# Retention and FFN on one core: two key casts on another engine, and one step's outputs inside an output block

## The chip, the cores and the metric

One core of one Trainium2 chip. A core has five engines with an instruction stream of their own: TensorE (PE; its weight loads are listed as PEld), VectorE (DVE), ScalarE (ACT), GpSimd (POOL) and SyncE (SP), which here only issues DMAs. Each works its stream strictly in order; between engines, semaphores hold an instruction until what it needs is done. The metric is the device time of one execution in microseconds, as a median over runs.

## The reference

A decaying linear attention (retention), 4 batches of 8 heads, 768 tokens, head width 64, followed by a multiplicative feed-forward network on the 3072 tokens:

```python
for t in range(S):
    state = gamma[None, :, None, None] * state + np.einsum('bhd,bhe->bhde', k[:, :, t], v[:, :, t])
    y[:, :, t] = scale * np.einsum('bhd,bhde->bhe', q[:, :, t], state)
...
a = x @ w1            # x: (3072, 512), from y; w1, w2: (512, 1024)
b = x @ w2
h = a * b @ w3        # w3: (1024, 1024)
return (h @ w_out)    # w_out: (1024, 512)
```

## The kernel before

**Tiles.** The sequence is cut into 24 chunks of 128 tokens (`n`; six per batch). In a chunk the recurrence is done as matrices: `scores(n)` multiplies keys and queries (L437) into two PSUM banks, VectorE multiplies each by the causal mask into `am` (L442); `kv(n)` makes the chunk's addition to the state (L460), VectorE adds the old state (L468) and GpSimd scales (L469); `outputs(n)` adds masked scores times values (L477, L478) and state times queries (L480) in one bank, which VectorE scales into the transposed FFN input `xt` (L485). Decay factors are folded into the scaled values `vp`, the factors `YS` and the state scale `GS`.

The keys enter the scores transposed. `transposes(n)` fills `kp` (L426 and L230 from TensorE's transposes, L411 and L412 from a DMA transpose). The DMA makes it for chunk 6 and for chunks from 8 on (`by_dma`), the rest TensorE.

**The FFN.** w3 and w_out are multiplied into one matrix `W3O` in the prologue, so a block of tokens needs `a_unit` (w1, L508, then a ScalarE copy, L518), `b_unit` (w2, L508, then a VectorE product with it into `ht`, L524) and `o_unit`: eight matmuls against `W3O` (L534), a ScalarE eviction (L539) and a DMA to the output (L541). `o_unit` takes an optional function `between`, called after the fourth matmul. Most blocks have 256 tokens; the second and third have 128.

**Order.** All order is written by hand (manual schedule). The first four chunks are unrolled with the weight preparation (the prologue); from chunk 4 on `step(n)` runs, with FFN units kept in a queue `fill`, from which it pulls a share by cost at three places. In step 5 the first unit that is pulled after `outputs(5)` is the output block of `ffn[1]`.

**Around the first edit.** The keys and values of chunks 2 and 3 come as one load for the pair, token pairs side by side in a partition. `pair_casts(n, moved, names, eng)` casts the half that stays on its partitions (by default on GpSimd) and the half that moves to the other 64 (by default on VectorE): for keys one copy of 64 partitions by 512 elements (L313), for values two multiplications (L318). In the prologue (L729 to L731) both chunks' keys are cast, then TensorE has the next matmuls of w1 (L719), the query transposes (L366), three more w1 blocks, and `transposes(2)`, which needs both halves of chunk 2. TensorE then goes on with w1, the transposes of chunk 3, `scores(2)`, the first part of w2 and `outputs(2)`. The two value multiplications on VectorE stand between the two masks of `scores(2)`; GpSimd does four in the meantime (two each for chunks 2 and 3).

**Around the second edit.** In step 5 TensorE has `scores(5)`, one `b_unit`, `outputs(5)`, the output block of `ffn[1]`, `scores(6)`, and FFN units of the next block, which read `xt` of chunks 4 and 5. `transposes(6)` issues no TensorE work: it is the two ScalarE copies L411 and L412, from the DMA transpose that step 4 issued.

Of the kernel before, what the change touches and what calls it, by code (L numbers as in the profile page):

```python
# [18 lines left out]
def kernel(  # L19
# [11 lines left out]
    nc = tc.nc  # L31
# [210 lines left out]
    def bank(tag, shape, dtype, name):  # L242
        return (ps_t if tag == "psT" else ps_at).tile(shape, dtype, tag=tag, name=name)
# [59 lines left out]
    def pair_casts(n, moved, names="kv", eng=None):  # L303

        m, c = divmod(n, 2)
        rows = slice(c * 64, c * 64 + 64)
        t = 1 - c if moved else c
        to = slice(t * 64, t * 64 + 64)
        eng = eng or (nc.vector if moved else nc.gpsimd)
        if n not in k16s:  # L310
            k16s[n] = att.tile([128, 512], HP, tag="k16", name="k16", bufs=3)
        if "k" in names:
            eng.tensor_copy(  # L313
                k16s[n][to, :].rearrange("i (h d) -> i h d", d=D),
                pair_in["k", m][rows, :].rearrange("i (h t d) -> i h t d", t=2, d=D)[:, :, t, :],
            )
        for r in range(2 if "v" in names else 0):
            eng.tensor_tensor(  # L318
                VP[n % 3][to, :, r, r * 64 : r * 64 + 64],
                pair_in["v", m][rows, :].rearrange("j (p s t e) -> j p s t e", s=2, t=2, e=64)[:, :, r, t, :],  # L320
                VS2[rows, t, :].rearrange("j (p s) -> j p s", s=2)[:, :, r].unsqueeze(2).broadcast_to((64, NP, 64)),
                MULT,
            )
# [9 lines left out]
    def casts(n):  # L333
        if n >= NSTEP:
            return
        k32, v32 = chunk_in.pop(n)
        if n % 2 == 0:
            q_cast(n // 2)
        k16 = att.tile([128, 512], HP, tag="k16", name="k16", bufs=3)
        nc.gpsimd.tensor_copy(k16[:, :], k32[:, :])  # L340
        vp = VP[n % 3]

        for r in range(2):
            nc.gpsimd.tensor_tensor(  # L344
                vp[:, :, r, r * 64 : r * 64 + 64],
                v32[:, :].rearrange("j (p s e) -> j p s e", s=2, e=64)[:, :, r, :],
                VS[:, :].rearrange("j (p s) -> j p s", s=2)[:, :, r].unsqueeze(2).broadcast_to((128, NP, 64)),
                MULT,
            )
        k16s[n] = k16  # L350
# [30 lines left out]
    def by_dma(n):  # L381

        return n >= DT0 and n != DT0 + 1

    def dma_transposes(n):

        if n < DT0 or n >= NSTEP:
            return
        if by_dma(n):
            kT = att.tile([128, NP, 128], HP, tag="kT", name="kT", bufs=2)  # L390
            nc.sync.dma_start_transpose(kT[:, :, :], k16s[n][:, :])
            kTs[n] = kT
        if n % 2 == 0:
            qT = att.tile([128, 2, NP, 128], HP, tag="qTd", name="qTd", bufs=2)
            nc.sync.dma_start_transpose(
                qT[:, :, :, :].rearrange("p t a i -> p (t a) i"), q16s.pop(n // 2)[:, :]
            )
            qTd[n // 2] = qT

    def queries(n, p):  # L400
        if n < DT0:
            return qTs[n][:, p, :]
        c = n % 2
        return qTd[n // 2][:, :, p, c * 64 : (c + 1) * 64]

    def transposes(n, tag="psT"):
        if n >= NSTEP:
            return
        if by_dma(n):
            kT, kp = kTs.pop(n), KP[n % 2]  # L410
            nc.scalar.copy(kp[0:64, :, 0, :], kT[0:64, :, :])  # L411
            nc.scalar.copy(kp[64:128, :, 1, :], kT[64:128, :, :])  # L412
            return
        transposes_front(n, tag)
        transposes_back(n)

    def transposes_front(n, tag):
        k16 = k16s[n]
        ps = bank(tag, [128, NP, 128], HP, "psT")
        for p in range(NP):  # L420
            nc.tensor.transpose(ps[:, p, :], k16[:, p * 128 : (p + 1) * 128], ident16[:, :])
        kTs[n] = ps

    def transposes_back(n):
        kp, ps = KP[n % 2], kTs.pop(n)
        nc.scalar.copy(kp[0:64, :, 0, :], ps[0:64, :, :])  # L426
        cast_to(kp[64:128, :, 1, :], ps[64:128, :, :], False)

    def scores(n, tags=("psA0", "psA1"), between=None):
        kp = KP[n % 2]  # L430
        am = att.tile([128, NP, 2, 128], HP, tag="am", name="am")
        for half in range(2):
            ps = bank(tags[half], [128, 2, 2, 128], FP, "psA")
            for i in range(2):
                p = half * 2 + i
                for r in range(2):
                    nc.tensor.matmul(  # L437
                        ps[:, i, r, :], lhsT=kp[:, p, r, :], rhs=queries(n, p), start=True, stop=True
                    )
            if half and between:  # L440
                between()
            nc.vector.tensor_tensor(  # L442
                am[:, half * 2 : half * 2 + 2, :, :].rearrange("j p s i -> j (p s) i"),
                ps[:, :, :, :].rearrange("j p s i -> j (p s) i"),
                (keep2 if n < 4 else keep)[:, :].unsqueeze(1).broadcast_to((128, 4, 128)),
                MULT,
            )
        ATs[n] = am

    def kv(n, tag="psK", eng=nc.gpsimd):  # L450
        k16, vp = k16s.pop(n), VP[n % 3]
        c = n % NCH
        if c == NCH - 1:
            return None
        ps = bank(tag, [128, NP, 128], FP, "psK")
        for p in range(NP):

            rhs = vp[:, p, :, :].rearrange("j s e -> j (s e)")
            rhs = bass.AP(rhs.tensor, rhs.offset, [list(rhs.ap[0]), [192, 2], [1, 64]])
            nc.tensor.matmul(  # L460
                ps[:, p, :], lhsT=k16[:, p * 128 : (p + 1) * 128], rhs=rhs, start=True, stop=True
            )
        t16 = att.tile([128, NP, 128], HP, tag="t16", name="t16")
        if c == 0:
            nc.vector.tensor_tensor(t16[:, :, :], ps[:, :, :], GS[:, :, :], MULT)
        else:
            s32 = att.tile([128, NP, 128], FP, tag="s32", name="s32")
            nc.vector.tensor_tensor(s32[:, :, :], ps[:, :, :], Tst[0][:, :, :], ADD)  # L468
            eng.tensor_tensor(t16[:, :, :], s32[:, :, :], GS[:, :, :], MULT)  # L469
        return t16  # L470

    def outputs(n, tag="psY"):
        am, vp = ATs.pop(n), VP[n % 3]
        c = n % NCH
        ps = bank(tag, [128, NP, 128], FP, "psY")
        for p in range(NP):
            nc.tensor.matmul(ps[:, p, :], lhsT=vp[:, p, 0, :], rhs=am[:, p, 0, :], start=True, stop=False)  # L477
            nc.tensor.matmul(ps[:, p, :], lhsT=vp[:, p, 1, :], rhs=am[:, p, 1, :], start=False, stop=(c == 0))  # L478
            if c > 0:
                nc.tensor.matmul(ps[:, p, :], lhsT=Tst[0][:, p, :], rhs=queries(n, p), start=False, stop=True)  # L480
        if n % 2 == 0:
            XT[n // 2] = xpool.tile([128, NP, 256], HP, tag="xt", name="xt")

        order = "p a (t i) -> p a t i"
        nc.vector.tensor_tensor(  # L485
            XT[n // 2][:, :, n % 2 * C : (n % 2 + 1) * C].rearrange("p a (i t) -> p a t i", t=2),
            ps[:, :, :].rearrange(order, t=2), YS[:, :, :].rearrange(order, t=2), MULT,
        )
# [107 lines left out]
    fill = Queue()  # L596
# [3 lines left out]
    def step(n):  # L600

        ready = n * C
        share = fill.available(ready) / (2 - n % 2)
        if n >= DT0 - 2:
            casts(n + 2)
        scores(n)
        fill.pull(share * 0.25, ready)
        t_new = kv(n)
        if n < DT0 - 2:
            casts(n + 2)  # L610
        dma_transposes(n + 2)
        load_chunk(n + 4)
        if n % 2:
            q_transposes((n + 1) // 2)
        if n == 4:
            transposes(5)
        fill.pull(share * 0.25, ready)
        outputs(n)
        Tst[0] = t_new
        if n != 4:  # L620
            transposes(n + 1)
        fill.pull(share * 0.5, ready)

# [44 lines left out]
    cast_w3(7, w3_st[7])  # L668
    q_cast(0)
    pair_casts(0, False, "k")  # L670
    pair_casts(1, False, "k")
    pair_casts(0, False, "v")
# [28 lines left out]
    ffn = [Ffn(a, b - a) for a, b in zip(bounds, bounds[1:])]  # L701
# [26 lines left out]
    by_rows(W1, ps, 1)  # L728
    for n in (2, 3):  # L729
        pair_casts(n, False, "k")  # L730
        pair_casts(n, True, "k")  # L731
    by_rows(W1, ps, 2)
    q_back = q_transposes(1, True)
    q_back(0)
# [92 lines left out]
```

## Time and profile before

| | |
|---|---|
| median of 10 runs | 196.7 us (195.85 to 198.07) |
| the profiled execution | 196.37 us |
| its span (first to last recorded instruction) | 194.3 us |
| TensorE busy, share of the span | 186.2 us, 96% |
| VectorE busy | 118.0 us, 61% |
| ScalarE busy | 99.0 us, 51% |
| GpSimd busy | 85.7 us, 44% |
| moved by DMA | 40.54 MB, 209 GB/s mean |

A row of a timeline has the start in us from the span's start, the length in us, engine, source line, operation, what is written and read, the shape, and how many such instructions are merged; in brackets, how long the engine sat idle before it, and what ended that. The releaser is inferred: where the engine named had long been done, it was something else, often a DMA. Matmuls overlap in the pipeline, so the starts of two that follow each other say what one costs: 0.055 us for 128 columns, 0.216 for 512 here.

### The profile page before, as it was taken

The page shows a single profiled execution, that of the slowest core. Times are in us where ns is not written, and L with a number is a line of the kernel's source. Part 1 is how long each engine was busy: PE and PEld are TensorE (multiplying, and loading weights), DVE is VectorE, ACT ScalarE, POOL GpSimd, SP SyncE. Part 2 cuts the span into 40 slices and gives each one's busy share as a digit, 9 for nine tenths or more (in the row PEclk, how much of TensorE's full clock was granted, in tenths as well). Part 3 has the DMA queues.
Part 4 walks back from the last instruction along what each step waited for, and adds up shares of the span by engine and source line. Part 5 has one row for each costly group of instructions (what it writes and reads, how often), then busy time and mean ns, then how long its engine had stood idle before and what let it go on. Part 6 is the DMA issues. An engine that isn't in the chain of part 4 may idle for free.

```text
span 194.3 us, 4696 instructions
## 1 busy us (share of the span) xinstructions
PE 186.2 (96%) x1777; PEld 141.0 (73%) x1777; DVE 118.0 (61%) x221; ACT 99.0 (51%) x191; POOL 85.7 (44%) x146
## 2 busy tenths in 40 slices
PE   6899999779999999999999999999999999999993
PEld 2445567568796889778877887788778877887752
DVE  3225498699586768657565766575657665753220
ACT  5478465582444455455545554555455545533322
POOL 7600378738764747385242643852426432200000
PEclk9999999999999999999999999999999999999999
DMA  6999999999999999999999989969979931111104
GB/s 206 360 390 392 301 399 320 366 284 220 210 180 233 211 235 243 170 242 209 267 189 189 212 186 224 207 155 255 204 182 198 206 95 25 57 54 54 43 29 148
DMA packets 85030, 40.54 MB, mean 209 GB/s; under 512 B 61328, under 2 KB 80016, under 8 KB 85008
## 3 DMA queue, kind: packets, MB, share of 16 engines
q1 hardware_dynamic: 85008, 40.25, 88.2%
q8 instruction: 14, 0.23, 0.5%
q14 instruction: 8, 0.07, 0.2%
HBM read 29.36 MB, written 6.29 MB: 184 GB/s over the span
## 4 chain that ended last, share of the span: by engine, by line
PE 84%; DMA 7%; DVE 3%; ACT 3%; POOL 1%; issue 1%; SPq 0%; POOLq 0%
PE psF L508 39%; PE psO L534 20%; DMA stg<-in_moe_w_dram 7%; PE psA L437 5%; PE psW L280 3%; PE psY L477 3%; PE psY L478 2%; PE psY L480 2%; PE psK L460 2%; PE psW L259 1%; PE psZ L634 1%; DVE am L442 1%; ACT w L230 1%; PE psF L719 1%; PE psW L293 1%; PE psG L508 1%
## 5 line engine op out<-in xcount | busy, mean ns | idle before, releaser
L508 PE MATMUL psF<-xt,w 128*128 128x256 f16 (+1 forms) x736 | 85.0, 266 | 0.0
L508 PEld LDWEIGHTS <-w 128*128 128x128 f16 x768 | 68.2, 98 | 7.2
L524 DVE TENSOR_TENSOR ht<-pa,psF 128x256 f16<-128x256 f32 x88 | 36.6, 416 | 22.1 <-PE psF L508 12.9
L518 ACT COPY pa<-psF 128x256 f32<-128x256 f32 x84 | 31.3, 372 | 33.8 <-PE psF L508 33.3
L442 DVE TENSOR_TENSOR am<-psA,keep 128x512 f16<-128x512 f32 x48 | 31.0, 685 | 22.9 <-PE psA L437 22.8
L534 PE MATMUL psO<-w3o,ht 128*128 128x512 f16 x184 | 43.1, 379 | 0.0
L469 POOL TENSOR_TENSOR t<-s,GS 128x512 f16<-128x512 f32 x15 | 19.3, 1284 | 43.0 <-DVE s L468 38.8
L539 ACT ACTIVATE osb<-psO 128x512 f32<-128x512 f32 x23 | 13.7, 597 | 37.5 <-PE psO L534 37.5
L534 PEld LDWEIGHTS <-ht 128*128 128x128 f16 x184 | 17.9, 98 | 17.2 <-DVE ht L768 0.2
L344 POOL TENSOR_TENSOR vp<-v,VS 128x256 f16<-128x256 f32 x40 | 23.8, 617 | 5.2 <-PE psY L478 2.2
L327 POOL CAST q<-q 128x1024 f16<-128x1024 f32 x12 | 12.7, 1057 | 24.2 <-DMA q<-in_q_dram 24.2
L485 DVE TENSOR_TENSOR xt<-psY,YS 128x512 f16<-128x512 f32 x24 | 17.8, 743 | 3.5 <-PE psY L480 3.2
L477 PE MATMUL psY<-am,vp 128*128 128x128 f16 x96 | 16.8, 219 | 0.9 <-ACT kp L230 0.5
L478 PE MATMUL psY<-am,vp 128*128 128x128 f16 x96 | 16.7, 219 | 0.4 <-DVE vp L318 0.4
L437 PEld LDWEIGHTS <-kp 128*128 128x128 f16 x192 | 12.5, 98 | 4.9 <-ACT kp L230 0.9
L340 POOL CAST k<-k 128x512 f16<-128x512 f32 x20 | 12.3, 614 | 5.3 <-PE psK L460 2.3
L468 DVE TENSOR_TENSOR s<-psK,t 128x512 f32<-128x512 f32 x16 | 11.0, 688 | 3.0 <-PE psK L460 2.7
L251 DVE COPY w3t<-psW 128x1024 f16<-128x1024 f16 x8 | 5.4, 688 | 11.1 <-PE psW L259 8.7
L437 PE MATMUL psA<-qTd,kp 128*128 128x128 f16 x144 | 11.1, 219 | 0.0
L480 PE MATMUL psY<-qTd,t 128*128 128x128 f16 x60 | 10.8, 219 | 0.0
L411 ACT COPY kp<-kT 64x512 f16<-64x512 f16 x17 | 10.5, 618 | 0.6 <-DMA kT<-k 0.2
L478 PEld LDWEIGHTS <-vp 128*128 128x128 f16 x96 | 9.4, 98 | 1.9 <-POOL vp L318 0.9
(80 smaller groups left out, 195.6 us busy)
## 6 DMA issues: line engine op xcount, KB each, us to landing
stg<-in_moe_w_dram SPq DMA_DIRECT2D x16, 512.0 KB, 7.9
q<-in_q_dram SPq DMA_DIRECT2D x12, 512.0 KB, 5.4
out_dram<-osb SPq DMA_DIRECT2D x23, 256.0 KB, 2.5
k<-in_k_dram SPq DMA_DIRECT2D x20, 256.0 KB, 5.2
v<-in_v_dram SPq DMA_DIRECT2D x20, 256.0 KB, 5.1
stg<-in_moe_w_out_dram SPq DMA_DIRECT2D x4, 512.0 KB, 7.8
stg<-in_k_dram SPq DMA_DIRECT2D x2, 512.0 KB, 10.7
stg<-in_v_dram SPq DMA_DIRECT2D x2, 512.0 KB, 8.2
```

The lines of the kernel that those rows point to most:

```text
L344: nc.gpsimd.tensor_tensor(vp[:, :, r, r * 64 : r * 64 + 64], v32[:, :].rearrange("j (p s e) -> j p s e", s=2, e=64)[:, :, r, :], VS[:, :]. ...
L437: nc.tensor.matmul(ps[:, i, r, :], lhsT=kp[:, p, r, :], rhs=queries(n, p), start=True, stop=True)
L442: nc.vector.tensor_tensor(am[:, half * 2 : half * 2 + 2, :, :].rearrange("j p s i -> j (p s) i"), ps[:, :, :, :].rearrange("j p s i -> j ( ...
L469: eng.tensor_tensor(t16[:, :, :], s32[:, :, :], GS[:, :, :], MULT)
L477: nc.tensor.matmul(ps[:, p, :], lhsT=vp[:, p, 0, :], rhs=am[:, p, 0, :], start=True, stop=False)
L478: nc.tensor.matmul(ps[:, p, :], lhsT=vp[:, p, 1, :], rhs=am[:, p, 1, :], start=False, stop=(c == 0))
L480: nc.tensor.matmul(ps[:, p, :], lhsT=Tst[0][:, p, :], rhs=queries(n, p), start=False, stop=True)
L485: nc.vector.tensor_tensor(XT[n // 2][:, :, n % 2 * C : (n % 2 + 1) * C].rearrange("p a (i t) -> p a t i", t=2), ps[:, :, :].rearrange(orde ...
L508: nc.tensor.matmul(ps[:, i * w : (i + 1) * w], lhsT=W[d][:, (f + i) * 128 : (f + i + 1) * 128], rhs=XT[self.tok0 // TB][:, d, c0 : c0 + w] ...
L518: nc.scalar.copy(self.pa[f][:, :], ps[:, :])
L524: nc.vector.tensor_tensor(self.HT[:, f : f + TB // self.width, :].rearrange("p f n -> p (f n)"), self.pa.pop(f)[:, :], ps[:, :], MULT,)
L534: nc.tensor.matmul(psO[:, :], lhsT=self.HT[:, f, tb * 128 : (tb + 1) * 128], rhs=W3O[f][:, :], start=(f == 0), stop=(f == 7),)
```

## The change

Two edits. The moved key halves of chunks 2 and 3 are cast by ScalarE instead of VectorE. In step 5, the head of the queue (the output block of `ffn[1]`) is taken out and run at once, with `outputs(5)` and `transposes(6)` called between its fourth and fifth matmul; before, they stood in front of it.

```diff
         if "k" in names:
-            eng.tensor_copy(
+            (nc.scalar.copy if eng is nc.scalar else eng.tensor_copy)(
                 k16s[n][to, :].rearrange("i (h d) -> i h d", d=D),
...
         fill.pull(share * 0.25, ready)
-        outputs(n)
+        if n == 5:
+
+            fill.units.pop(0)
+            ffn[1].o_unit(0, lambda: [outputs(n), transposes(6)])
+        else:
+            outputs(n)
         Tst[0] = t_new
-        if n != 4:
+        if n not in (4, 5):
             transposes(n + 1)
         fill.pull(share * 0.5, ready)
...
     for n in (2, 3):
         pair_casts(n, False, "k")
-        pair_casts(n, True, "k")
+        pair_casts(n, True, "k", nc.scalar)
     by_rows(W1, ps, 2)
```

In the built program, VectorE's stream loses the two copies, ScalarE's has them ahead of the key copies of chunk 2 (L426), and TensorE's has the first four matmuls of the output block ahead of the twelve of `outputs(5)`. The streams of GpSimd and SP are as before.

## The prediction

> **What bounds the kernel now.** I read the chain of work that ended last first, then the two places that the change touches in order of time, then the durations of single instructions. The page:
>
> ```profile
> PE   6899999779999999999999999999999999999993
> ...
> PEclk9999999999999999999999999999999999999999
> ...
> PE 84%; DMA 7%; DVE 3%; ACT 3%; POOL 1%; issue 1%; SPq 0%; POOLq 0%
> ```
>
> TensorE is the bound, at a clock that never drops. From 62 us on the waits list only 0.2 us for TensorE, so what it gains before that reaches the end unless something new becomes late. It stands open in few places; both edits lie in one of them. First place, the end of the prologue (chunk 2), by time:
>
> ```profile
> 34.81 1.17 DVE L313 CAST k<-stg 64x512 f16<-64x512 f32 x2 [1.56 <-DMA stg<-in_k_dram]
> 34.84 0.86 POOL L313 CAST k<-stg 64x512 f16<-64x512 f32 x1 [0.69 <-PE psTq L366]
> 35.76 0.40 PE L421 MATMUL psT<-ident,k 128*128 128x128 f16 x4 [0.58 <-POOL k L313]
> 36.25 0.58 ACT L426 COPY kp<-psT 64x512 f16<-64x512 f16 x1 [3.68 <-PE psT L421]
> 37.49 0.56 PE L437 MATMUL psA<-qT,kp 128*128 128x128 f16 x7 [0.38 <-ACT kp L230]
> 37.87 0.69 DVE L442 TENSOR_TENSOR am<-psA,keep 128x512 f16<-128x512 f32 x1 [0.62 <-PE psA L437]
> 37.88 0.61 POOL L318 TENSOR_TENSOR vp<-stg,VS 64x256 f16<-64x256 f32 x1 [0.32 <-PE psA L437]
> 40.13 0.69 DVE L442 TENSOR_TENSOR am<-psA,keep 128x512 f16<-128x512 f32 x1
> 40.88 0.22 PE L477 MATMUL psY<-am,vp 128*128 128x128 f16 x1 [0.19 <-DVE am L442]
> ```
>
> The reader should see one chain: GpSimd's half of the key cast (ends 35.70) releases the transposes, these the key copies on ScalarE, these the scores, these VectorE's mask (L442); behind it VectorE scales two value halves (38.59 to 40.10), masks the second half, and only then can TensorE finish the outputs of chunk 2. The value scaling is slow, as its instructions one by one show (each row from a short stretch of time; min/median/max ns, first and last start):
>
> ```profile
> L318 POOL TENSOR_TENSOR vp<-stg,VS x2: 608/608/609, 37.9 to 38.5; 64x256 f16<-64x256 f32 x2
> L318 DVE TENSOR_TENSOR vp<-stg,VS x1: 756/756/756, 38.6 to 38.6; 64x256 f16<-64x256 f32 x1
> L318 POOL TENSOR_TENSOR vp<-stg,VS x1: 686/686/686, 39.1 to 39.1; 64x256 f16<-64x256 f32 x1
> L318 DVE TENSOR_TENSOR vp<-stg,VS x1: 832/832/832, 39.3 to 39.3; 64x256 f16<-64x256 f32 x1
> L318 DVE TENSOR_TENSOR vp<-stg,VS x6: 419/794/1489, 26.2 to 44.3; 64x256 f16<-64x256 f32 x6
> ```
>
> Alone it takes VectorE 0.42 us (the smallest of six); here 0.76 and 0.83. The two engines take turns: GpSimd's four run 37.88, 38.49, 39.10, 39.79, and VectorE's two end some 0.25 and 0.31 us after GpSimd's second and third do (39.35, 40.10). Second place, step 5:
>
> ```profile
> 58.36 1.29 DVE L442 TENSOR_TENSOR am<-psA,keep 128x512 f16<-128x512 f32 x2
> 58.38 0.61 PE L508 MATMUL psF<-xt,w 128*128 128x128 f16 x8
> 59.10 0.22 PE L477 MATMUL psY<-am,vp 128*128 128x128 f16 x1
> 59.70 0.22 PE L477 MATMUL psY<-am,vp 128*128 128x128 f16 x1
> 60.03 1.89 PE L534 MATMUL psO<-w3o,ht 128*128 128x512 f16 x8
> ```
>
> One unit of 8 matmuls doesn't cover the two masks: TensorE waits for each half.
>
> **Part 1, the two key casts go from VectorE to ScalarE.** VectorE loses two instructions (1.17 us), ScalarE gains two ahead of L426; no other order changes. ScalarE has been idle since 32.56 (3.68 us), so nothing of its own is queued in front; behind them wait L426 and, through it, the scores.
>
> What they cost there is not in the trace. Near rows:
>
> ```profile
> L230 ACT CAST w<-stg x5: 1041/1046/1048, 30.0 to 41.8; 128x1024 f16<-128x1024 f32 x5
> ...
> 39.63 1.99 ACT L230 CAST w<-stg 128x1024 f16<-128x1024 f32 x2
> ...
> L411 ACT COPY kp<-kT x17: 617/618/619, 58.7 to 167.7; 64x512 f16<-64x512 f16 x17
> ```
>
> L411 has the size and both sides in SBUF: 0.61 us I take for one. Two weight casts in a row take 1.99, not 2.09, so the second starts 0.10 early: 0.51 + 0.61 = 1.12 us, from 34.83 to 35.95. Low bound 0.59 each (the 128x512 copy from PSUM), high bound 1.05 each (the whole 1024-wide cast).
>
> The Trainium skill speaks against the move: "ScalarE: Activation LUTs", Rules for kernel authors, budgets about 0.3 us plus 0.83 ns an element for an activation with a pointer bias, and prefers VectorE for simple work. By that one cast is 0.3 + 0.42 = 0.72 us, the pair ends at 36.27, and L426 starts at 36.29, no earlier than now: part 1 is then worth nothing. I go by the L411 row, a plain copy of the same size on this chip.
>
> What is gained is GpSimd's cast. Its first took 0.86 while VectorE cast beside it, against 0.607 at the least. "SBUF — State Buffer", Who interferes with whom, says that GpSimd and a VectorE cast in a two-port mode, or one with two SBUF inputs, share a port pair that is held for a whole instruction, and that ScalarE never waits there; the alternation above is this lock. Without VectorE's casts GpSimd's ends at 34.84 + 0.61 = 35.45, as does ScalarE's first. Then: transposes 35.51 (0.06 later, as now), their end 35.91, L426 at 36.00 (0.09 later, as now; ScalarE is free at 35.95). That is 0.25 earlier than 36.25, and the scores follow (ScalarE's two copies are a fixed 1.2 us), so the mask runs 37.62 to 38.31. The transposes of chunk 3 need GpSimd's second cast, 36.06, before TensorE is there at 36.28. VectorE's query copies, freed at 34.9, were not what the scores waited for.
>
> Now the lock. GpSimd's scaling starts at 37.88 whatever happens: it waits for the landing of the values (issued at 31.21, 6.6 us to landing, 37.8). VectorE's first scaling arrives at 38.34 instead of 38.59. GpSimd's second starts at 38.49. Arriving 0.15 us ahead of it, VectorE gets the turn one place earlier: it ends at 38.49 + 0.25 = 38.74; GpSimd's second is stretched to 0.69 like the third now (39.17); VectorE's second ends 39.17 + 0.31 = 39.48. That is 40.10 - 39.48 = **0.62 us** earlier. The second mask starts at 39.51 and TensorE's second half of the outputs at 40.26 instead of 40.88. The first half needs the key copies of chunk 3 out of its bank (39.60 now, 39.35 then): not late. Had VectorE arrived between 38.49 and 39.10, it would end at 40.10 as now and part 1 would give 0. Between these ends I take 0.62.
>
> From there VectorE runs without a gap to 48.9 and TensorE nearly so, both 0.62 earlier. The weight casts on ScalarE (first 39.63, then 39.38) stay ahead of their matmuls at 41.04.
>
> **Part 2, outputs of chunk 5 between the 4th and 5th matmul of the output block.** The same 12 + 8 matmuls; only TensorE's order changes. The four copies and transfers that are named with it keep their place on ScalarE and SP: chunk 6's keys come by DMA, so its key copies are ScalarE work that stood in front of the block's eviction before, too. The block's bank is free once VectorE's product at 57.88 is done (58.28), before the masks. In starts: the unit begins at 58.38 and takes 8 x 0.055 = 0.44, to 58.82; half a block 1.73/2 = 0.87, to 59.69; outputs 12 x 0.055 = 0.66 (both masks done at 59.65), to 60.35; other half to 61.22. Now the block ends at 60.03 + 1.73 = 61.76: **0.54 us** gained. The output evacuation by VectorE (L485) moves from 60.23 to about 60.39, relative to the next scores (61.22) still early: it ends at 61.1, and its first reader starts at 61.67. If that cover were gone, the next unit would wait.
>
> **What is late next.** With 1.16 us gone, the scores of chunk 6 come at 61.76 - 1.16 = 60.60. Their key copies wait for a DMA transpose (0.21 at 58.72) and end at 59.97; their queries land at 55.47 + 4.0 = 59.5. That leaves 0.6 us if the DMA side doesn't move at all. Chunk 9's keys, issued at 71.93 and some 3.6 us under way, would start their copies at 75.58, needed at 78.86. So nothing is taken back.
>
> **Sum** against the profiled execution: 196.37 us around a span of 194.3, less 0.62 and 0.54: 195.21, span 193.1. That execution is 0.33 below the median 196.7, so for the median 196.7 - 1.16 = 195.5.
>
> **Rivals.**
> A: VectorE's first scaling misses the turn. For it: the margin is 0.15 us, out of two DMA landings and an unmeasured cast; the skill's 0.72 alone would do it. Against: the L411 row. Only part 2 counts: 196.7 - 0.54 = 196.2.
> B, slower: ScalarE's cast, which moves partitions and reads with a stride, takes as long as the 1024-wide one. At c us each the pair ends at 34.83 + 2c - 0.10, L426 starts 2c - 1.50 later than now, and beyond c = 1.0 the arrival passes 39.10, GpSimd's third comes first, and 0.69 is lost: 196.7 + 0.69 - 0.54 = 196.85. Past 39.79 (c = 1.35) another 0.69: 197.5. Against: no ScalarE row of this size is over 0.62.
> C: part 2 is hidden, because the copies of chunk 6's keys or its queries come late once TensorE is early: 196.7 - 0.62 = 196.1. Against: the 0.6 us above.
> D: neither does anything: 196.7.
>
> **How the numbers follow.** Forecast 0.47, A 0.27, B 0.10 (0.05 of it past the second turn), C 0.08, D 0.08. Measurement can tell about 0.5%, 1.0 us. Faster by that means under 195.7: the forecast, less the share in which it comes out small, and a little of A and C, 0.48. Slower is the far end of B and what I don't see, 0.09; the rest is the same, 0.43. The range goes from 194.9 (the forecast and one more turn of 0.6 won from GpSimd in a later stretch) to 196.85, the near end of B; the forecast's own is 195.1 to 195.9.
>
> **What would show it.** Right: GpSimd's L313 at 0.61 twice; the new ScalarE casts at about 0.6; VectorE's first L318 of chunk 2 ahead of GpSimd's second; 40.88 becomes about 40.3; no gap in front of the output block in step 5. Wrong: L426 still at 36.25 or later; VectorE's L318 pair still ending near 40.1; the scores of chunk 6 waiting for ScalarE or the query transpose.

## The result, and the profile after

The changed kernel takes 195.05 us (median of 14 runs, 194.82 to 196.09) against 196.37 us for the kernel before (51 runs beside them). The ratio is 0.9933, 95% interval 0.9917 to 0.9949: 1.3 us faster, between 1.0 and 1.6 by the interval. A second set of runs gave 0.9938 (0.9919 to 0.9957). The forecast was 1.16 us less; from the 196.37 of these runs that is 195.2, ratio 0.9941. The profiled execution took 195.13 us around a span of 193.3 us.

The page of the changed kernel, its span, TensorE's row of tenths and the chain by engine:

```profile
span 193.3 us, 4697 instructions
...
PE   6899999889999999999999999999999999999993
...
PE 83%; DMA 6%; POOL 3%; SPq 2%; ACT 2%; issue 1%; DVE 1%; ACTq 0%; POOLq 0%
```

TensorE is still the bound; two slices of the prologue went from 7 tenths to 8. The end of the prologue, by time (start, length, engine, line, what, idle before):

```profile
34.94 1.26 ACT L313 CAST k<-stg 64x512 f16<-64x512 f32 x2 [2.28 <-DMA stg<-in_k_dram]
34.97 1.28 POOL L313 CAST k<-stg 64x512 f16<-64x512 f32 x2 [0.70 <-PE psTq L366]
35.70 0.38 PE L421 MATMUL psT<-ident,k 128*128 128x128 f16 x4 [0.41 <-POOL k L313]
36.18 0.58 ACT L426 COPY kp<-psT 64x512 f16<-64x512 f16 x1
37.42 0.56 PE L437 MATMUL psA<-qT,kp 128*128 128x128 f16 x7 [0.38 <-ACT kp L230]
37.79 0.69 DVE L442 TENSOR_TENSOR am<-psA,keep 128x512 f16<-128x512 f32 x1 [0.72 <-PE psA L437]
39.72 0.69 DVE L442 TENSOR_TENSOR am<-psA,keep 128x512 f16<-128x512 f32 x1
40.46 0.22 PE L477 MATMUL psY<-am,vp 128*128 128x128 f16 x1 [0.19 <-DVE am L442]
```

The keys landed 0.13 us later in this execution (34.94 for 34.81), so times are best counted from there. The first mask came 2.85 us after the landing instead of 3.06, a gain of 0.21; the second came 4.78 after it instead of 5.32, a gain of 0.54. The 0.33 between them was won in the value scaling. Its instructions one by one (short stretches of time; min/median/max ns, first and last start):

```profile
L318 POOL TENSOR_TENSOR vp<-stg,VS x1: 609/609/609, 38.0 to 38.0; 64x256 f16<-64x256 f32 x1
L318 DVE TENSOR_TENSOR vp<-stg,VS x1: 418/418/418, 38.5 to 38.5; 64x256 f16<-64x256 f32 x1
L318 POOL TENSOR_TENSOR vp<-stg,VS x1: 824/824/824, 38.6 to 38.6; 64x256 f16<-64x256 f32 x1
L318 DVE TENSOR_TENSOR vp<-stg,VS x1: 829/829/829, 38.9 to 38.9; 64x256 f16<-64x256 f32 x1
```

GpSimd's second scaling as a row of the timeline, in the kernel before and in the changed one:

```profile
38.45 0.61 POOL L318 TENSOR_TENSOR vp<-stg,VS 64x256 f16<-64x256 f32 x1
...
38.58 0.82 POOL L318 TENSOR_TENSOR vp<-stg,VS 64x256 f16<-64x256 f32 x1
```

VectorE's first scaling now starts at 38.52, 0.06 us ahead of GpSimd's second. It takes 0.42 us, its time when alone, and it is GpSimd's second that is stretched, to 0.82 us. Before, VectorE (38.59) came 0.13 us behind GpSimd's second and was itself held. Step 5, in the timeline of the changed kernel:

```profile
57.95 1.29 DVE L442 TENSOR_TENSOR am<-psA,keep 128x512 f16<-128x512 f32 x2
57.97 0.61 PE L508 MATMUL psF<-xt,w 128*128 128x128 f16 x8
58.42 1.03 PE L534 MATMUL psO<-w3o,ht 128*128 128x512 f16 x4
58.68 0.62 ACT L411 COPY kp<-kT 64x512 f16<-64x512 f16 x1 [0.58 <-DMA kT<-k]
59.28 0.22 PE L477 MATMUL psY<-am,vp 128*128 128x128 f16 x1
59.95 1.03 PE L534 MATMUL psO<-w3o,ht 128*128 128x512 f16 x4
60.82 0.61 PE L437 MATMUL psA<-qTd,kp 128*128 128x128 f16 x8
```

TensorE goes from the FFN unit into the output block (58.42), from there into the outputs (59.28, 0.86 later, as half a block takes) and back (59.95, 0.67 later) with no wait. From the scores of chunk 5 (57.53) to those of chunk 6 it is 3.29 us; it was 57.93 to 61.76, 3.83 us.

### The profile page after: what moved, and what is told of

Its sections match the earlier page's. It is cut to its first block, busy times and chain, and to the rows that moved or that the text cites. A ratio compares the mean times of both kernels' runs of the same rounds, so it can differ in the third digit from the quotient of the medians.

```text
span 193.3 us, 4697 instructions
## 1 busy us (share of the span) xinstructions
PE 185.2 (96%) x1777; PEld 140.2 (73%) x1777; DVE 117.0 (61%) x219; ACT 100.2 (52%) x193; POOL 85.4 (44%) x146
## 4 chain that ended last, share of the span: by engine, by line
PE 83%; DMA 6%; POOL 3%; SPq 2%; ACT 2%; issue 1%; DVE 1%; ACTq 0%; POOLq 0%
PE psF L508 39%; PE psO L534 21%; DMA stg<-in_moe_w_dram 6%; PE psA L437 5%; PE psW L293 3%; PE psY L477 3%; PE psY L478 2%; SPq L62 2%; PE psF L724 2%; PE psY L480 2%; PE psK L460 2%; POOL vp L318 2%; PE psG L508 1%; PE psO L551 1%; PE psW L268 1%
## 5 line engine op out<-in xcount | busy, mean ns | idle before, releaser
L442 DVE TENSOR_TENSOR am<-psA,keep 128x512 f16<-128x512 f32 x48 | 30.9, 684 | 22.1 <-PE psA L437 22.0
L411 ACT COPY kp<-kT 64x512 f16<-64x512 f16 x17 | 10.5, 618 | 1.0 <-DMA kT<-k 0.6
L412 ACT COPY kp<-kT 64x512 f16<-64x512 f16 x17 | 10.5, 615 | 0.4
```

The source lines that it names most:

```text
L442: nc.vector.tensor_tensor(am[:, half * 2 : half * 2 + 2, :, :].rearrange("j p s i -> j (p s) i"), ps[:, :, :, :].rearrange("j p s i -> j ( ...
```

## The experiments

Two accounts of part 1 are to be told apart. The *turn* theory: VectorE and GpSimd take turns with the value scalings (at a shared port, in the prediction's reading), and what pays is that VectorE arrives before GpSimd's second one. The *plain-chain* theory: every step simply starts a little earlier. For part 2: the block *fills* two waits, or its gain is given back later. Two intervals are read off every profile: from the start of the first key cast to chunk 2's second mask, and from the scores of chunk 5 to those of chunk 6. Each ratio is to runs of the kernel before that stood beside it; their medians lie between 196.33 and 196.37.

| kernel | cast to second mask | scores 5 to scores 6 | median | ratio to before, interval |
|---|---|---|---|---|
| before | 34.81 to 40.13: 5.32 | 3.83 | 196.37 | |
| changed | 34.94 to 39.72: 4.78 | 3.29 | 195.05 | 0.9933 (0.9917 to 0.9949) |
| casts alone | 35.36 to 40.15: 4.79 | 3.82 | 195.89 | 0.9982 (0.996 to 1.0005) |
| outputs alone | 35.05 to 40.40: 5.35 | 3.29 | 195.93 | 0.9979 (0.9965 to 0.9993) |
| changed, VectorE late | 34.87 to 40.19: 5.32 | 3.29 | 195.62 | 0.9973 (0.9964 to 0.9982) |
| before, VectorE late | 34.94 to 40.19: 5.25 | 3.82 | 196.23 | 0.9998 (0.9985 to 1.0011) |
| before, GpSimd gap | 34.74 to 39.72: 4.98 | 3.82 | 195.75 | 0.9974 (0.996 to 0.9989) |
| changed, outputs after two | (values landed late) | 3.39 | 195.19 | 0.9959 (0.9933 to 0.9985) |
| changed, key copies split | 35.02 to 39.85: 4.83 | 3.29 | 195.21 | 0.995 (0.9933 to 0.9967) |

### The casts alone

```diff
-        pair_casts(n, True, "k")
+        pair_casts(n, True, "k", nc.scalar)
```

(against the kernel before; the copy inside `pair_casts` is as in the change)

> Only the two key casts move to ScalarE; step 5 is as before. Turn theory (VectorE's first value scaling comes before GpSimd's second and so wins a whole turn of the shared port): second mask 0.4 us earlier than before, as in the changed kernel, time 0.4 to 0.6 us below the kernel before (ratio 0.997 to 0.998). Plain-chain theory (only the key copies start earlier, by 0.07 us in the changed kernel's profile): 0.1 us, ratio 0.9995. The step 5 gap of TensorE stays.

The timeline of this kernel:

```profile
35.36 1.26 ACT L313 CAST k<-stg 64x512 f16<-64x512 f32 x2 [2.17 <-DMA stg<-in_k_dram]
...
38.43 2.74 POOL L318 TENSOR_TENSOR vp<-stg,VS 64x256 f16<-64x256 f32 x4 [0.62 <-PE psA L437]
...
38.94 1.17 DVE L318 TENSOR_TENSOR vp<-stg,VS 64x256 f16<-64x256 f32 x2
...
40.15 0.69 DVE L442 TENSOR_TENSOR am<-psA,keep 128x512 f16<-128x512 f32 x1
```

The loads were half a microsecond late in this execution, so 40.15 looks like no gain; counted from the cast, the mask comes 0.53 us earlier than before, as in the changed kernel. VectorE's pair takes 1.17 us instead of 1.51. The time is 0.35 us lower (0.8 lower to 0.1 higher): in keeping with 0.5, but the measured time alone would not show it.

### The outputs alone

```diff
-        pair_casts(n, True, "k", nc.scalar)
+        pair_casts(n, True, "k")
```

(against the changed kernel)

> Only step 5's outputs move into the output block; the casts stay on VectorE. Fill theory: TensorE's two waits in step 5 go, 0.54 us below the kernel before (ratio 0.997), the prologue as before. If the gain were given back at the scores of chunk 6 (late key copies or queries): ratio 0.999 to 1.0 and a wait in front of those scores.

Timeline of step 5:

```profile
59.10 1.03 PE L534 MATMUL psO<-w3o,ht 128*128 128x512 f16 x4
59.44 0.62 ACT L411 COPY kp<-kT 64x512 f16<-64x512 f16 x1 [0.66 <-DMA kT<-k]
...
60.63 1.03 PE L534 MATMUL psO<-w3o,ht 128*128 128x512 f16 x4
61.50 0.61 PE L437 MATMUL psA<-qTd,kp 128*128 128x128 f16 x8
```

The step takes 3.29 us, 0.54 less than before, with no wait in front of the scores of chunk 6. The prologue is as before (5.35). The time is 0.41 us lower (0.14 to 0.69). In the profiles the two parts add up: 0.53 us in one kernel, 0.54 in the other, and 0.54 twice in the changed kernel. The measured times neither show nor exclude it: 0.18% and 0.21% are 0.39%, against the changed kernel's 0.67%, and the three intervals are wide enough for both.

### VectorE a little later, in both kernels

The same zero fill on VectorE, behind the first mask of chunk 2, put into the changed kernel and into the one before:

```diff
-    scores(2, between=lambda: pair_casts(2, True, "v"))
+    late = const.tile([128, 256], FP, name="late")
+    scores(2, between=lambda: [nc.vector.memset(late[:, :], 0.0), pair_casts(2, True, "v")])
```

> The changed kernel with a zero fill of 128x256 on VectorE (about 0.27 us) between the first mask of chunk 2 and the value scaling. Turn theory: VectorE now arrives after GpSimd's second scaling has started, so the pair ends about 0.55 us later than in the changed kernel (at 40.2 for 39.7), twice the fill; time 0.5 us above the changed kernel, ratio to the kernel before 0.996. Plain-chain theory: 0.27 us later at most, ratio 0.9947.

> The kernel before with the same fill of about 0.27 us in the same place. Turn theory: VectorE arrives at 38.86 instead of 38.59, still between GpSimd's second and third start (38.49, 39.10), so the pair ends at 40.1 as before and the time is the same, ratio 1.000. Plain-chain theory: 0.27 us later, ratio 1.0014.

Timeline of the changed kernel with the fill:

```profile
37.94 2.70 POOL L318 TENSOR_TENSOR vp<-stg,VS 64x256 f16<-64x256 f32 x4 [0.60 <-PE psA L437]
...
38.51 0.61 POOL L318 TENSOR_TENSOR vp<-stg,VS 64x256 f16<-64x256 f32 x1
...
38.42 0.27 DVE L753 MEMSET late<- 128x256 f32 x1
38.72 1.44 DVE L318 TENSOR_TENSOR vp<-stg,VS 64x256 f16<-64x256 f32 x2
...
40.19 0.69 DVE L442 TENSOR_TENSOR am<-psA,keep 128x512 f16<-128x512 f32 x1
```

and of the kernel before with it:

```profile
37.90 2.74 POOL L318 TENSOR_TENSOR vp<-stg,VS 64x256 f16<-64x256 f32 x4 [0.22 <-DMA stg<-in_v_dram]
...
38.68 0.27 DVE L748 MEMSET late<- 128x256 f32 x1
38.98 1.18 DVE L318 TENSOR_TENSOR vp<-stg,VS 64x256 f16<-64x256 f32 x2
...
40.19 0.69 DVE L442 TENSOR_TENSOR am<-psA,keep 128x512 f16<-128x512 f32 x1
```

The same 0.27 us costs 0.54 us in one kernel (4.78 to 5.32) and nothing in the other (5.32 to 5.25; counted from GpSimd's first scaling, 2.25 to 2.29). In the first it pushes VectorE from ahead of GpSimd's second scaling to behind it (38.72 against 38.51). In the second VectorE was behind it anyway, and the fill only takes up time that VectorE spent waiting. A plain chain would have paid 0.27 in both. With the fill the changed kernel's ratio, 0.9973 (0.996 was expected), is close to that of the outputs alone, 0.9979: part 1's gain is gone, though ScalarE still does the casts.

### More work on GpSimd, in the kernel before

```diff
         for r in range(2 if "v" in names else 0):
+            if r and gap:
+                gap()
...
-    pair_casts(2, False, "v")
+    late = const.tile([128, 256], FP, name="late")
+    pair_casts(2, False, "v", gap=lambda: nc.gpsimd.memset(late[:, :], 0.0))
```

> The kernel before, casts on VectorE, with a zero fill of 128x256 added on GpSimd between its first and second value scaling of chunk 2 (about 0.3 us more work). Turn theory: GpSimd's second scaling now starts after VectorE's arrival at 38.59, VectorE wins the turn, its second mask starts 0.2 to 0.3 us earlier than before although only work was added: ratio about 0.999, and the step from GpSimd's first scaling to the second mask shrinks from 2.25 us to about 2.0. Plain-chain theory: VectorE waits for nothing of GpSimd's order, the mask stays where it is or comes up to 0.3 us later.

Its timeline (L320 and L444 are L318 and L442 of the kernel before):

```profile
37.80 0.61 POOL L320 TENSOR_TENSOR vp<-stg,VS 64x256 f16<-64x256 f32 x1 [0.31 <-PE psA L439]
...
38.35 0.30 POOL L745 MEMSET late<- 128x256 f32 x1
38.52 1.18 DVE L320 TENSOR_TENSOR vp<-stg,VS 64x256 f16<-64x256 f32 x2
38.62 2.12 POOL L320 TENSOR_TENSOR vp<-stg,VS 64x256 f16<-64x256 f32 x3
...
39.72 0.69 DVE L444 TENSOR_TENSOR am<-psA,keep 128x512 f16<-128x512 f32 x1
```

With the casts still on VectorE and 0.30 us of useless work added to GpSimd, the second mask comes 1.92 us after GpSimd's first scaling instead of 2.25, and the kernel is faster: 0.9974, with 1 outside the interval. That is the turn without the change: GpSimd's second scaling (38.62) now comes behind VectorE's arrival (38.52). The 0.33 us that the profile shows is less than the 0.51 of the ratio, but inside its interval (0.2 to 0.8).

### Half the fill

```diff
-    def o_unit(self, tb, between=None):
+    def o_unit(self, tb, between=None, at=4):
...
-                if f == 4 and between:
+                if f == at and between:
...
-            ffn[1].o_unit(0, lambda: [outputs(n), transposes(6)])
+            ffn[1].o_unit(0, lambda: [outputs(n), transposes(6)], 2)
```

> The changed kernel with the outputs of chunk 5 after two instead of four matmuls of the block. Fill theory: two matmuls cover 0.43 us, the first mask's wait (0.28) goes whole, of the second's (0.27) some 0.1 stays: scores of chunk 5 to scores of chunk 6 take 3.4 us instead of 3.29, against 3.83 in the kernel before; time 0.1 us above the changed kernel, not to be told from it by the clock. If the place within the block mattered otherwise (bank, late xt), the step is 3.29 or less, or above 3.6.

Timeline of step 5:

```profile
59.44 0.59 PE L534 MATMUL psO<-w3o,ht 128*128 128x512 f16 x2
59.87 0.22 PE L477 MATMUL psY<-am,vp 128*128 128x128 f16 x1
60.04 0.22 PE L477 MATMUL psY<-am,vp 128*128 128x128 f16 x1
60.31 0.22 PE L477 MATMUL psY<-am,vp 128*128 128x128 f16 x1
...
61.94 0.61 PE L437 MATMUL psA<-qTd,kp 128*128 128x128 f16 x8
```

Two heads of the outputs follow each other by 0.17; from the second to the third it is 0.27, so 0.10 is left of the wait for the second mask, and the step takes 3.39 us (58.55 to 61.94). What counts is the length of the work put into the wait. The measured time doesn't tell it from the changed kernel (195.19 against 195.17 in the repeat):

> The changed kernel unaltered, on the chip and beside the runs of the next three, to compare them with it: ratio 0.9933 again (0.9917 to 0.9949).

The repeat gave 0.9938 (0.9919 to 0.9957), its second mask 4.78 us behind the cast again. In the profiled execution with two matmuls the values of chunk 2 landed at about 39.5 instead of 38.0, so both engines' scalings began there. VectorE's came 0.05 us ahead of GpSimd's first, and its pair took 1.17 us, as when it wins a turn; the table's first interval can't be compared.

### A step further that gave nothing

The second half of chunk 2's key copies goes to VectorE, which idles there:

```diff
-    def transposes_back(n):
+    def transposes_back(n, on_dve=False):
...
-        cast_to(kp[64:128, :, 1, :], ps[64:128, :, :], False)
+        cast_to(kp[64:128, :, 1, :], ps[64:128, :, :], on_dve)
...
-    transposes(2)
+    transposes_front(2, "psT")
+    transposes_back(2, True)
```

> The changed kernel, and the second half of the key copies of chunk 2 on VectorE (idle there) instead of behind the first half on ScalarE. The scores of chunk 2 come 0.5 us earlier. Turn theory: what that is worth depends on who is first when the values land; VectorE's arrival near 38.0 is level with GpSimd's first scaling. If VectorE comes first, the second mask is 0.6 us earlier than in the changed kernel (ratio 0.990), if it comes just after, 0.1 us (ratio 0.993). Plain-chain theory: 0.5 us whatever the order.

Timeline:

```profile
36.26 0.58 ACT L426 COPY kp<-psT 64x512 f16<-64x512 f16 x1
...
36.87 0.43 DVE L228 COPY kp<-psT 64x512 f16<-64x512 f16 x1 [0.88 <-ACT kp L426]
...
37.33 0.69 DVE L228 COPY stg<-psF 128x512 f32<-128x512 f32 x1
...
37.94 0.68 DVE L442 TENSOR_TENSOR am<-psA,keep 128x512 f16<-128x512 f32 x1
...
59.81 0.62 ACT L411 COPY kp<-kT 64x512 f16<-64x512 f16 x1 [1.57 <-DMA kT<-k]
```

My expectation missed two things. The built program makes VectorE's copy wait for ScalarE's, so the halves still go one after the other. And VectorE's own copy of an FFN bank (0.69 us), which used to fit into the pause before the mask, stands behind it now and delays the mask. The second mask is 4.83 us behind the cast, for 4.78; the time is that of the changed kernel (195.21 for 195.17). VectorE still came ahead of GpSimd's second scaling (38.65 for 38.68), so neither theory is tested by it.

## Why the prediction was right

**Part 1, ScalarE's cast.** The row of the key copies was the right guide: 0.617 us for each cast, between the bounds of 0.59 and 1.05. It is below the 0.72 that the prediction estimated from the budget of the Trainium skill ("ScalarE: Activation LUTs", Rules for kernel authors). That budget is for an activation with a pointer bias, and these are plain copies. With 0.72 each VectorE would have missed the turn: by estimate, 0.2 us later than it came, where its lead was 0.06. The 0.10 us of overlap that two weight casts show was not had: the pair takes 1.26 us, not 1.12. The second cast has waits of its own in the program (for VectorE and GpSimd), where the second weight cast carries one; that this is the reason was not tried. The 0.10 is no constant either: the same two weight casts take 2.06 us in the changed kernel instead of 1.99. So ScalarE, not TensorE, released L426, 1.24 us after the landing instead of 1.44, a gain of 0.20 for 0.25.

**GpSimd's cast** went from 0.86 to 0.61 us, as forecast from the smallest row, and with VectorE's casts gone nothing held it.

**The turn** is the step on which the forecast stood or fell (rival A was its failure), and three runs show it: a small delay of VectorE lost it in one kernel, cost nothing in the other, and a delay of GpSimd won it in the kernel before. The waiting lies inside the rows: VectorE's second scaling and GpSimd's second wait for no semaphore, and the engine that started first keeps the length it has alone. That the thing in dispute is a port is the prediction's reading of the page that it cites; no run here tells it from another resource that only one of the two can have.

The size was forecast as 0.62 and is 0.54 us, counted from either landing. The prediction took each start on GpSimd for the end of the scaling before it (38.49, 39.10); the rows start at 38.45 and 39.14. So VectorE's two scalings ended 0.28 us behind GpSimd's second and third, both of them, and not 0.25 and 0.31. Two terms of the sum were off besides. VectorE arrived 0.51 us after GpSimd's first scaling began (38.01 to 38.52), not 0.46. And GpSimd's second, now the one that waits, ended 0.47 us behind VectorE's first (39.41 for 38.94), where the sum gave it 0.43 (39.17 for 38.74). These lose 0.09, VectorE's first 0.02 more (0.42 us for 0.40), and the 0.28 for 0.31 gives back 0.03.

That the turn was won was in part luck. The forecast's margin was 0.15 us; from the rows it was 0.11 (38.34 for 38.45), and it came out as 0.06. The margin hangs on when the values land after the keys. From the first key cast to GpSimd's first scaling it was 3.06 to 3.10 us in eight of the ten profiles. In the kernel before with the fill it was 2.96; by estimate (2.96 + 0.57 against the 3.58 from cast to VectorE) such a landing puts VectorE 0.04 us behind GpSimd's second in the changed kernel. How often that happens was not measured.

**Part 2** is right to the hundredth: 0.54 us, in the changed kernel and alone.

**What is late next.** The transposed keys of chunk 6 did not move with TensorE, as the prediction had allowed for: ScalarE's copies of them began at 58.68, for 58.72. They end at 59.93, 0.9 us ahead of the scores. But that landing varies: the copies began at 60.06 in the kernel with the casts alone and at 59.81 with the key copies split, where they end at 61.06 and TensorE's weight loads for the scores wait 0.27 us for them. The scores then take TensorE 0.57 us from their start to the next unit instead of 0.44, so 0.13 us is lost there. So rival C is a matter of single executions; in the other profiles it cost nothing.

**The sum.** The spans differ by 1.0 us (194.3 to 193.3): 0.54 and 0.54 less the 0.13 by which the loads came later. The profiled executions differ by 1.24, since what lies around the span was 2.07 before and 1.83 after. The forecast of 1.16 and the 1.08 of the two profiled gains both lie inside the measured interval of 1.0 to 1.6; what more the median of 1.3 may hold was not looked for.

## What to carry to other kernels

When the instructions of two engines hold each other up whole, as the scalings do here, the price of an edit can come in whole turns: write down when each engine arrives and where the other's instructions begin, and ask on which side of such a border the edit puts it. A quarter of a microsecond can then be worth half of one or nothing, and delaying the engine that isn't critical can pay. A wait inside an in-order stream is closed by putting work of the same length, which is ready, in front of the waiting instruction; its worth is the length of the waits, read from the starts.

## What was not expected of the hardware

**Two figures give every held row of these scalings.** In all ten profiles a scaling that starts while one of the other engine is under way is held, save in the last 0.1 us of a GpSimd row (next paragraph). The closest starts were a lead of VectorE of 0.03 us, which sufficed (38.65 for 38.68, in the kernel with the key copies split), and one of GpSimd of 0.10, which did too (38.73 for 38.83, in the outputs alone); what lies between was not measured. A VectorE scaling that is held ends 0.28 us after GpSimd's, wherever it started: started 0.13 us behind GpSimd's it took 0.76 us, started 0.21 behind it took 0.68. A GpSimd scaling that is held ends 0.47 or 0.48 us after VectorE's. The key casts before the change fit too: VectorE's first ended at 35.23 and GpSimd's at 35.70, VectorE's second at 35.98.

**A VectorE scaling that starts just before the end of a GpSimd one is not held.** Started 0.10 us before that end (38.52 against 38.62), it took 0.418 us, and so it did in the kernel before with the fill (38.98, GpSimd's second ending at 39.08), where GpSimd's third was then stretched to 0.72 us. The Trainium skill ("SBUF — State Buffer", Who interferes with whom) has the port pair held for a whole instruction. These rows don't contradict it. Of its 0.42 us VectorE needs only the last 0.28 after GpSimd is done, so by estimate it can start up to 0.14 us before GpSimd's end and lose nothing. The other reading, that GpSimd lets go before its row ends, was not told from this.

And useless work on GpSimd, 0.30 us, made the kernel 0.26% faster.
